# Splitting w_out by GpSimd ahead of time, through a spare tile and DRAM, in a fused attention and gated-MLP block

## The chip, the cores and the metric

The kernel runs on one core of a Trainium2 chip. The time is device microseconds (us) of one execution on that core; several executions were timed, and one further execution was taken by the hardware profiler. The engines are named as on the profile's page: PE (TensorE, matrix products), PEld (its weight loads), DVE (VectorE), ACT (ScalarE), POOL (GpSimd) and SP (SyncE, which here only issues transfers). A name with a q (SPq) is that engine's sequencer.

## What is computed

```python
x = A_x                                                # 1 x 2048 x 640, float32
h = x + _A_ref(_layernorm(x), A_wqkv, A_wo)            # 32 heads of 20, sliding window of 256
z = gelu(layernorm(h) @ w_in)                          # 2048 x 1728
z1, z2 = z[..., :864], layernorm(z[..., 864:])
g = w_sp @ z2 + b_sp[:, None]                          # w_sp: 2048 x 2048, over positions
h2 = h + (z1 * g) @ w_out                              # w_out: 864 x 640
```

Products want nearly full float32 accuracy. So the kernel writes an operand as a sum of two parts, a rounded "hi" (type fp32r) and the rest "lo" = raw - hi, and makes three products for one: hi x hi, hi x lo and lo x hi. To **split** a tile is to make these two parts.

## The kernel before

There are 16 row tiles of 128 positions. The attention half ends at about 550 us. Then come four stages, all written as a list of steps: `steps.append((products, what follows them))`, and `at(n, f)` hangs a piece of work f on step n.

- **z stage**, 64 steps (`z_pair`): z1 for all 16 tiles, from normalized rows that are read back from DRAM (`hn_d`). Rows of the last tiles (`hn(14)`, `hn(15)`) lie in `rows[2]` and `rows[3]`.
- **z2 stage, first five pairs**, 20 steps (`z2_pair(8..12)`): the second half of z (products `zb`), its layernorm, and `right_blocks`, which makes from it the seven pieces per block that a Strassen-like product with seven products instead of eight needs. Pieces are in tiles `ze` and `zl`. A part of these element-wise operations is given to GpSimd (`eng` = `nc.gpsimd`). The fifth pair is computed ahead and kept in DRAM (`z2_d`).
- **gate, opening half**, 56 steps (`first_gate`): the first 8 column tiles of w_sp times the pieces, products `g`, kept in DRAM as `g_d`. During it `staged_pieces` lets GpSimd alone make the seven pieces of the fifth pair through the spare tile `stage` [128, 2, 432]: load, copy (hi), subtract (lo), store to `zp_d`. SP loads them from there (lines 1019 and 1020).
- **z2, last three pairs**, 12 steps, **then the gate's second half**, 56 steps (`second_gate(0..7)`): products `g` again, added to `g_d`, times z1, turned (`turn_y`, products `yt_ps`), and projected with w_out (`final`, products `out_ps`).

The split w_out lies in `e1["wout"]`, in the memory that `win2` (the split w_in of the z2 stage) leaves at the last `zb` product. In the kernel before, `second_gate(0)` fills it: for each of the seven 128-row blocks, SP loads the raw block into `stage` (k < 4) or `rows[3]`, ACT copies it to the hi part (L136) and DVE subtracts (L137). Then `stage` and `rows[1]` serve as the two tiles of h that the result is added to (`load_h`, L1137).

The order within each engine in these stages is not written by hand. It is made when the program is built, by a scheduler that replays the steps on an estimated time line. So the same source lines can come in another order where the work around them changes. Every engine then takes its instructions strictly in that order, SP its transfers too.

Of the kernel before, what the change touches and what calls it, by code (L numbers as in the profile page):

```python
# [7 lines left out]
F32 = mybir.dt.float32  # L8
# [7 lines left out]
P = 128  # L16
S = 2048
D = 640
H = 32
DH = 20  # L20
NT = S // P
KD = D // P
FH = 864
KF = 7
HF = FH // 2
# [9 lines left out]
def block_kernel(ctx, tc, x, wqk, wv, wo, w_in, wsp, bsp, w_out, out):  # L35
    nc = tc.nc
# [4 lines left out]
    def pool(stack, name, **kw):  # L41
        return stack.enter_context(tc.tile_pool(name=name, bufs=1, reuse_waits="tile", **kw))

    const = pool(ctx, "const")
    dram = pool(ctx, "dram", space=DRAM)
# [12 lines left out]
    z2_d = dram.tile([2, P, FH], F32, name="z2_d")  # L58
    t_d = dram.tile([2, P, HF], F32, name="t_d")
    zp_d = dram.tile([7, P, 2, HF], F32, name="zp_d")  # L60

    ident = const.tile([P, P], F32, name="ident")
    nc.gpsimd.memset(ident, 1.0)
# [45 lines left out]
    def view(flat, lo, *shape):  # L109
        n = 1  # L110
        for d in shape:
            n *= d
        names = "abcd"[:len(shape)]
        return flat[:, lo:lo + n].rearrange(f"p ({' '.join(names)}) -> p {' '.join(names)}",
                                            **dict(zip(names, shape)))
# [15 lines left out]
    def m1(lo, *shape):  # L131
        return view(mem["m1"], lo, *shape)

    def split(hi, lo, raw, eng=None):

        nc.scalar.activation(hi, raw, AF.Copy)  # L136
        (eng or nc.vector).tensor_tensor(out=lo, in0=raw, in1=hi.bitcast(F32), op=OP.subtract)  # L137
# [91 lines left out]
    with ExitStack() as ab:  # L229
# [35 lines left out]
        minus = tmp2.tile([P, P], BF16, name="minus")  # L265
# [87 lines left out]
        def max_rows(g, b):  # L353


            n, cols, st = (40, 32)[b], m_cols.pop(b), slot_w[g % 3]
            m3 = tmp2.tile([P, 3, n], BF16, tag="m3", bufs=1, name=f"m3_{g}_{b}")
            mr = tmp2.tile([P, n], F32, tag="mr", bufs=1, name=f"mr{g}_{b}")
            nc.gpsimd.tensor_copy(out=m3[:, 0], in_=cols)
            nc.gpsimd.tensor_tensor(out=mr, in0=cols, in1=m3[:, 0], op=OP.subtract)  # L360
            nc.gpsimd.tensor_copy(out=m3[:, 1], in_=mr)
            nc.gpsimd.tensor_tensor(out=m3[:, 2], in0=mr, in1=m3[:, 1], op=OP.subtract)
            if b == 0:
                nc.gpsimd.tensor_copy(out=m_cols[1].rearrange("p (h r) -> p h r", h=4)[:, :, :2],
                                      in_=cols.rearrange("p (h r) -> p h r", h=4)[:, :, 8:])
            yield
            ps = s1_tile()[:3 * n, :P]
            nc.tensor.matmul(ps, m3.rearrange("p a c -> p (a c)"), minus, start=True, stop=True)
            mt = tmp2.tile([3 * n, P], BF16, tag="mt", bufs=1, name=f"mt{g}_{b}")
            nc.vector.tensor_copy(mt, ps)  # L370
            yield
            nc.sync.dma_start(st[b][0][120:123], mt.bitcast(F32))
            yield
# [86 lines left out]
        if True:  # L460
# [176 lines left out]
            for u in range(LEAD):  # L637
                for hh in range(4):
# [3 lines left out]
                    if (u, hh) in ((10, 0), (12, 2), (14, 0)):  # L642
                        rows = rows if u > 10 else max_rows(0, 0)
                        next(rows)
                    if (u, hh) == (NT, 0):
                        rows = max_rows(0, 1)
# [10 lines left out]
        for s in range(NU + 2):  # L657
# [7 lines left out]
            for hh in range(4):  # L665
# [4 lines left out]
                if hh == 0 and u1 <= NU and u1 % NT in (0, 10):  # L670
                    rows = max_rows((u1 - 1) // NT, 0 if u1 % NT else 1)
# [41 lines left out]
    def plus(out, a, b, op=OP.add, eng=None):  # L713
        (eng or nc.vector).tensor_tensor(out=out, in0=a, in1=b, op=op)  # L714

    def minus(out, a, b, eng=None):
        plus(out, a, b, OP.subtract, eng)
# [44 lines left out]
    def hn(i):  # L762
        if i % 4 < 2:
            return m1((4 + i % 2) * D, D)
        return rows[i % 4][:, :D] if i > 11 else view(fx, (i % 4 - 2 + i // 9 * 2) * D, D)

    def win_pieces(tiles):

# [39 lines left out]
    rows = [lp.tile([P, FH], F32, name=f"row{n}") for n in range(4)]  # L808
    stage = lp.tile([P, 2, HF], F32R, name="stage")
    tmp1 = lp.tile([P, 512], F32, name="tmp1")  # L810
    aw = lp.tile([P, 7168], F32R, name="aw")
    fx = lp.tile([P, 4096], F32, name="fx")
    win1 = win_pieces(zl)
    win2, zc, e1 = [], [], {}
# [31 lines left out]
    steps, later = [], {}  # L846

    def at(n, f):
        later.setdefault(n, []).append(f)
# [150 lines left out]
    def staged_pieces(n0, n1):  # L1000
        hi, raw = (stage.bitcast(F32)[:, k] for k in range(2))
        eng = nc.gpsimd
        b11, b12, b21, b22 = (z2_d[t, :, h * HF:(h + 1) * HF] for t in range(2) for h in range(2))

        def piece(m, src, less=None, keep=None):
            eng.dma_start(raw, src)
            if less is not None:
                eng.dma_start(hi, less)
                minus(raw, raw, hi, eng)
            if keep is not None:  # L1010
                eng.dma_start(keep, raw)
            eng.tensor_copy(out=stage[:, 0], in_=raw)
            minus(stage[:, 1], raw, hi, eng)
            eng.dma_start(zp_d[m], stage.bitcast(F32))

        for i, p in enumerate(((B11, b11), (T1, b12, b11, t_d[0]), (B21, b21), (T2, b22, t_d[0], t_d[1]), (B22, b22),
                               (T3, b22, b12), (T4, b21, t_d[1]))):
            at(n0 + 6 * i, lambda p=p: piece(*p))
        for i, m in enumerate((B11, T1, T2, B22, T3, B21, T4)):
            at(n1 + i + 1, lambda m=m: nc.sync.dma_start(zc[0][m].bitcast(F32), zp_d[m]))  # L1020

    e_start = []
    gbank = {}

# [108 lines left out]
    def tile_of(n):  # L1133
        return n // 2 + 8 * (n % 2)

    def load_h(n):
        nc.sync.dma_start(e1["h"][n % 2], h_d[tile_of(n)])  # L1137

    def final(n):
        ps = [bank("b", f"out_ps{n}_{j}") for j in range(2)]  # L1140
        project(ps, range(2), e1["y"])
        for j in range(2):
            final_half(ps, n, j, j == 1)
# [10 lines left out]
    def second_gate(p):  # L1154
        i, j = 2 * p, 2 * p + 1
        gi, gj = next(gate_rows), next(gate_rows)
        n0 = len(steps)
        if p == 0:
            at(n0, open_e1)
        g = {11: gi[:, :HF], 12: gi[:, HF:], 21: gj[:, :HF], 22: gj[:, HF:]}  # L1160

        def add(n):
            return lambda ps: plus(g[n], ps, g[n])

        def gated(n):
            t, c = (p + 8, j) if n > 20 else (p, i)
            z = e1["z1"][c % 2][:, HF * (n % 10 - 1):HF * (n % 10)]
            nc.vector.scalar_tensor_tensor(out=z, in0=g[n], scalar=bcol[:, t:t + 1], in1=z, op0=OP.add, op1=OP.mult)

        def load_z(n):  # L1170
            nc.sync.dma_start(e1["z1"][n % 2], z1_d[tile_of(n)])

        turns = (0, 1, 2, 3) if p > 1 else (0, 4, 4, 6)

        def extra(m):
            if p:
                for x, f in zip(turns, (lambda: turn_y(i - 2, e1["y"]), lambda: final(i - 2),
                                        lambda: turn_y(i - 1, e1["y"]), lambda: final(i - 1))):
                    if x == m:
                        f()  # L1180

        at(n0 - (0 if p else 1), lambda: nc.sync.dma_start(gi, g_d[p]))
        at(n0, lambda: nc.sync.dma_start(gj, g_d[p + 8]))
        at(n0 + (1 if p else 0), lambda: load_z(i))
        at(n0 + (turns[2] + 1 if p else 0), lambda: load_z(j))
        at(n0 + 4, lambda: gated(12))
        at(n0 + (6 if p == 1 else 5), lambda: gated(22))
        at(n0 + 6, lambda: gated(11))
        at(n0 + 7, lambda: gated(21))
        at(n0 + (9 if p == 0 else 6), lambda: load_h(i))  # L1190
        at(n0 + (11 if p == 0 else 7), lambda: load_h(j))
        gate_pair(p, 1, [add(11), add(22), add(12), add(12), add(22), add(11), add(21)], extra)
        if p == 0:
            def wout_raw(k):
                return e1["h"][0] if k < 4 else rows[3][:, :D]

            def load_wout(k):
                nc.sync.dma_start(wout_raw(k), w_out[k * P:(k + 1) * P, :])

            def put_wout(k):  # L1200
                split(e1["wout"][:, 0, k], e1["wout"][:, 1, k], wout_raw(k))

            for k in range(KF):
                t = n0 + (2 * k if k < 4 else 2 * k - 4)
                at(t, lambda k=k: load_wout(k))
                at(t + 2, lambda k=k: put_wout(k))

    for p in range(8):
        z_pair(p, 2 * p, 2 * p + 1, win1)
# [1 line left out]
        z2_pair(8 + p, p, p + 4, p)  # L1211
    z2_pair(12, 8, 12, 0, True)
    staged_pieces(len(steps) + 4, len(steps) + 49)
    for p in range(8):
        first_gate(p)
    for p in range(1, 4):
        z2_pair(12 + p, p + 8, p + 12, p)
    for p in range(8):
        second_gate(p)
# [56 lines left out]
    n = NT - 2  # L1276
# [34 lines left out]
```

## Time and profile before

| what | value |
|---|---|
| time, median of 3 runs | 1122.15 us (1116.82 to 1125.29) |
| profiled execution | 1121.05 us, its span 1119.3 us |
| PE busy | 1088.3 us, 97% of the span |
| DVE, ACT, POOL busy | 64%, 51%, 30% |
| granted TensorE clock | 0.998 of full |
| chain that ended last | PE 59%, DMA 5%, DVE 4%, ACT 2% |

Times in the views are us from the start of the span, durations in ns or us as marked. A view by stretches (windows) has one row for each stretch, with the busy time of each engine; the difference to the stretch's length is idle time. A timeline row has the start, the time from the first start to the last end, the engine, line, operation, tile written <- tiles read, and in brackets how long the engine had been idle and what ended that. The chain of waits is followed back from the last instruction.

### The profile page before, as it was taken

To read this page: it belongs to the slowest core of one execution; us is meant where nothing else is said; L and a number is where in the kernel's file an instruction comes from. 1 tells how busy PE (TensorE), PEld (TensorE's weight loads), DVE (VectorE), ACT (ScalarE), POOL (GpSimd) and SP (SyncE) were. 2 spreads that over 40 slices of the span, in tenths; PEclk is the share of its full clock that TensorE was granted. 3 is DMA by queue.
4 is the path that set the end of the run, shared out by engine and by line. 5 is a ranking of instruction groups with operands and counts; after the bars stand their busy time and mean duration, and the time that the engine had idled before them with its cause. 6 is when DMAs were issued, how large, how long until landed. Compare 5 with 4: busy or idle time off the path is not lost.

```text
span 1119.3 us, 27705 instructions
## 1 busy us (share of the span) xinstructions
PE 1088.3 (97%) x10667; PEld 976.1 (87%) x10667; DVE 715.4 (64%) x2038; ACT 573.9 (51%) x1222; POOL 336.4 (30%) x492
## 2 busy tenths in 40 slices
PE   8999999999999999989999999999999999999998
PEld 7998877668777887789989999999989899999998
DVE  6541113889999998676567478565538975566542
ACT  4334333259888999566766566433336521222210
POOL 3114444457666778401100155333101000000000
PEclk9999999999999999999999999999999999999999
DMA  7213665666666663588665421545571664444331
GB/s 259 74 33 102 171 218 165 204 208 196 194 198 192 209 194 119 170 277 288 226 200 177 151 76 38 182 153 197 177 248 38 202 182 140 124 135 148 99 95 59
DMA packets 86692, 182.44 MB, mean 163 GB/s; under 512 B 11552, under 2 KB 47904, under 8 KB 82640
## 3 DMA queue, kind: packets, MB, share of 16 engines
q1 hardware_dynamic: 82864, 169.46, 47.3%
q0 software_dynamic: 1392, 5.97, 1.6%
q10 hardware_dynamic: 2304, 5.24, 1.2%
q8 instruction: 84, 1.38, 0.5%
q14 instruction: 48, 0.39, 0.1%
HBM read 119.54 MB, written 62.29 MB: 162 GB/s over the span
## 4 chain that ended last, share of the span: by engine, by line
PE 59%; DMA 5%; DVE 4%; ACT 2%; issue 1%; SPq 1%; POOL 1%; DVEq 0%; ACTq 0%; POOLq 0%
PE g L1091 22%; PE out_ps L1130 8%; PE zb L953 7%; PE pv L432 5%; PE bank L338 4%; PE bank L404 4%; PE wo_ps L95 2%; PE zx L901 2%; PE zv L901 1%; PE zy L901 1%; PE yt_ps L1119 1%; DMA wraw<-w_in_in 1%; DMA fx<-w_in_in 1%; DVE zl L714 1%; DMA m<-r_d 1%
## 5 line engine op out<-in xcount | busy, mean ns | idle before, releaser
L407 ACT ACTIVATE pt<-bank 128x384 f32<-128x384 f32 (+2 forms) x512 | 200.2, 492 | 14.7 <-PE bank L404 10.9
L1091 PE MATMUL g<-zl,aw 128*128 128x432 f32 x768 | 172.4, 359 | 1.8 <-DVE zl L714 1.2
L720 ACT ACTIVATE aw<-fx 128x512 fp32r<-128x512 f32 (+2 forms) x160 | 93.0, 595 | 156.2 <-PE g L1091 98.7
L350 DVE CUSTOM_DVE_ANT_0 junk<-bank,strip 128x288 bf16<-128x288 f32 x392 | 157.7, 454 | 3.9 <-PE bank L338 2.4
L1091 PEld LDWEIGHTS g<-zl,aw 128*128 128x128 f32 x768 | 143.3, 188 | 9.1 <-DVE zl L714 1.8
L1091 PE MATMUL g<-ze,aw 128*128 128x432 f32 x576 | 133.8, 361 | 1.4 <-ACT aw L720 0.7
L432 PE MATMUL pv<-pt,v_sb 128*32 128x192 f32 (+3 forms) x1984 | 127.5, 321 | 3.0 <-DVE ot L448 1.3
L714 DVE TENSOR_TENSOR aw<-fx,aw 128x512 fp32r<-128x512 f32 (+2 forms) x152 | 98.7, 658 | 27.0 <-ACT aw L720 26.1
L1091 PEld LDWEIGHTS g<-ze,aw 128*128 128x128 f32 x576 | 107.2, 188 | 7.9 <-ACT aw L720 1.5
L404 PE MATMUL bank<-slot 123*32 123x288 bf16 (+5 forms) x1536 | 107.0, 280 | 2.8 <-ACT pt L407 1.3
L409 POOL TENSOR_SCALAR_AFFINE_SELECT pt<-pt 128x512 f32<-128x512 f32 x128 | 82.4, 644 | 49.6 <-ACT pt L407 48.5
L1130 PE MATMUL out_ps<-wout,y_sp 128*128 128x320 f32 (+1 forms) x630 | 95.9, 309 | 0.4 <-ACT y_sp L136 0.4
L953 PE MATMUL zb<-win,aw 128*128 128x432 f32 x480 | 95.4, 359 | 0.0
L1130 PEld LDWEIGHTS out_ps<-wout,y_sp 128*128 128x128 f32 (+1 forms) x630 | 94.0, 188 | 1.2 <-ACT y_sp L136 0.7
L953 PEld LDWEIGHTS zb<-win,aw 128*128 128x128 f32 x480 | 89.9, 188 | 4.9 <-DVE aw L714 0.4
L338 PE MATMUL bank<-slot 120*32 120x288 bf16 (+2 forms) x1264 | 87.7, 283 | 2.2 <-issue 1.2
L538 DVE TENSOR_TENSOR rest<-qk,sg 128x512 f32<-128x512 f32 x40 | 27.6, 691 | 86.5 <-ACT sg L536 86.5
L412 POOL TENSOR_SCALAR_AFFINE_SELECT pt<-pt 128x512 f32<-128x512 f32 x112 | 73.4, 655 | 0.0
L404 PEld LDWEIGHTS <-slot 123*32 123x32 bf16 x1536 | 53.6, 96 | 17.8 <-issue 6.9
L432 PEld LDWEIGHTS pv<-pt,v_sb 128*32 128x32 f32 x1984 | 60.2, 110 | 9.0 <-POOL pt L412 3.7
L541 POOL TENSOR_TENSOR sg<-rest,sg 128x512 bf16<-128x512 f32 x40 | 46.6, 1164 | 69.7 <-ACT sg L540 62.1
L714 DVE TENSOR_TENSOR row<-g,row 128x432 f32<-128x432 f32 x80 | 47.9, 602 | 27.9 <-PE g L1091 22.5
(210 smaller groups left out, 2158.3 us busy)
## 6 DMA issues: line engine op xcount, KB each, us to landing
fx<-wsp_in SPq DMA_DIRECT2D x32, 512.0 KB
slot<-qk_d SPq DMA_DIRECT2D x72, 200.0 KB
qk_d<-sg SPq DMA_DIRECT2D x32, 384.0 KB
slot<-qk_d SPq DMA_DIRECT2D x72, 160.0 KB
fx<-hn_d SPq DMA_DIRECT2D x32, 320.0 KB
o_d<-ot SPq DMA_DIRECT2D x64, 128.0 KB
z_d<-row SPq DMA_DIRECT2D x18, 432.0 KB
g_d<-row SPq DMA_DIRECT2D x16, 432.0 KB
```

What stands on the lines that cost most here:

```text
L338: nc.tensor.matmul(ps[32 * j:32 * j + 32, :n], part(st, half, 120, 0, hh, q0, 32), part(st, half, 120, 1, hh, lo + skip * j, n), start=Tru ...
L350: nc.vector.tensor_tensor_reduce(out=junk[:, :n], in0=ps[:, :n], in1=keep, scale=1.0, scalar=NEG, op0=OP.add, op1=OP.max, accum_out=m_cols ...
L404: nc.tensor.matmul(ps[32 * i:32 * i + 32, b:e], part(st, half, 123, 1, hh, k0, 32), part(st, half, 123, 0, hh, kb * P + b, e - b), start=T ...
L407: nc.scalar.activation(pt[:, hh, :n], ps[:, :n], AF.Exp, scale=SCALE)
L409: nc.gpsimd.affine_select(out=pt[:, :, :P], in_=pt[:, :, :P], pattern=[[0, 4], [1, P]], base=0, channel_multiplier=-1, compare_op=OP.is_ge ...
L412: nc.gpsimd.affine_select(out=pt[:, :, 256:], in_=pt[:, :, 256:], pattern=[[0, 4], [-1, P]], base=-1, channel_multiplier=1, compare_op=OP. ...
L432: nc.tensor.matmul(ps[32 * hh:32 * hh + 32, a - 512 * c:b - 512 * c], v_sb[:, kb, v0:v0 + 32], pt[:, hh, a - kb * P:b - kb * P], start=fir ...
L714: (eng or nc.vector).tensor_tensor(out=out, in0=a, in1=b, op=op)
L720: nc.scalar.activation(out, a, AF.Copy)
L953: nc.tensor.matmul(b[0][:, :HF], a[t][:, x, kk], win2[0][:, y, kk, h * HF:(h + 1) * HF], start=kk + x + y == 0, stop=kk == KD - 1 and x == 1)
L1091: nc.tensor.matmul(ps, w[m][x][:, k], zc[k][m][:, y], start=start and k + x + y == 0, stop=stop and k == 3 and x == 1, skip_group_check=True)
L1130: nc.tensor.matmul(ps[j][:, :HD], src[:w, a, k, :], e1["wout"][:w, b, k, j * HD:(j + 1) * HD], start=(k == 0 and a + b == 0), stop=(k == K ...
```

## The change

Four things are edited.

- A new function `staged_wout` makes both parts of 432 columns of w_out on GpSimd, through `stage`, in the manner of `staged_pieces`, and keeps them in a DRAM tensor `wout_d`. It is called for 11 chunks (ten of 432 columns, one of 160): seven at the z stage's steps 3, 11, ..., 51, four at the steps 130, 132, 134 and 136 (46 to 52 steps behind the 84 of the z and the first z2 stages, near the end of the gate's opening half), behind the seven staged pieces.
- `second_gate(0)` loads both parts of each block straight into `e1["wout"]`: seven transfers of 640 KB in place of seven of 320 KB, and no split.
- w_out is handed to the kernel as [128, 7 x 640], so that a chunk of columns is one run of memory in each partition.
- `hn(15)` lies in `stage` in place of `rows[3]`.

```diff
+    wout_d = dram.tile([P, 2, KF * D], F32, name="wout_d")
...
     def hn(i):
         if i % 4 < 2:
             return m1((4 + i % 2) * D, D)
-        return rows[i % 4][:, :D] if i > 11 else view(fx, (i % 4 - 2 + i // 9 * 2) * D, D)
+        if i == NT - 1:
+            return stage.bitcast(F32).rearrange("p a b -> p (a b)")[:, :D]
+        return rows[2][:, :D] if i == NT - 2 else view(fx, (i % 4 - 2 + i // 9 * 2) * D, D)
...
+    def staged_wout(c):
+        n = min(HF, KF * D - c)
+        hi, lo = (stage[:, k, :n] for k in range(2))
+        nc.gpsimd.dma_start(lo.bitcast(F32), w_out[:, c:c + n])
+        nc.gpsimd.tensor_copy(out=hi, in_=lo.bitcast(F32))
+        minus(lo, lo.bitcast(F32), hi.bitcast(F32), nc.gpsimd)
+        nc.gpsimd.dma_start(wout_d[:, :, c:c + n], stage.bitcast(F32)[:, :, :n])
...
         if p == 0:
-            def wout_raw(k):
-                return e1["h"][0] if k < 4 else rows[3][:, :D]
-
-            def load_wout(k):
-                nc.sync.dma_start(wout_raw(k), w_out[k * P:(k + 1) * P, :])
-
-            def put_wout(k):
-                split(e1["wout"][:, 0, k], e1["wout"][:, 1, k], wout_raw(k))
-
             for k in range(KF):
-                t = n0 + (2 * k if k < 4 else 2 * k - 4)
-                at(t, lambda k=k: load_wout(k))
-                at(t + 2, lambda k=k: put_wout(k))
+                at(n0 + 1 + 3 * k // 2, lambda k=k: nc.sync.dma_start(e1["wout"][:, :, k].bitcast(F32), wout_d[:, :, k * D:(k + 1) * D]))
...
+    for i, c in enumerate(range(0, KF * D, HF)):
+        at(3 + 8 * i if i < 7 else len(steps) + 32 + 2 * i, lambda c=c: staged_wout(c))
...
-    w_out = np.pad(np.asarray(B_w_out), ((0, KF * P - FH), (0, 0)))
+    w_out = np.pad(np.asarray(B_w_out), ((0, KF * P - FH), (0, 0))).reshape(KF, P, D).transpose(1, 0, 2)
+    w_out = w_out.reshape(P, KF * D)
```

The built programs show where this lands. The last number in a name is the tile's running number, which is one or more higher in the changed program, and line numbers grow by 1 to 11. First, DVE at the start of the gate's second half, where it makes the last pieces `zl` of the last z2 pair. Before:

```order
L714 TENSOR_TENSOR row2_9612<-row3_9613,row2_9612 128x432
L1168 SCALAR_TENSOR_TENSOR z1_0_13064<-row0_9610,bcol_81,z1_0_13064 128x432
L137 TENSOR_TENSOR wout_13062<-stage_9614,wout_13062 128x640
L714 TENSOR_TENSOR row3_9613<-row3_9613,row2_9612 128x432
L714 TENSOR_TENSOR zl11_9605<-row2_9612,zl11_9605 128x432
L714 TENSOR_TENSOR row1_9611<-g1_0_1_1_13097,row1_9611 128x432
L714 TENSOR_TENSOR aw_9616<-fx_9617,aw_9616 128x512
L714 TENSOR_TENSOR zl15_9609<-row3_9613,zl15_9609 128x432
```

The same place in the changed program:

```order
L715 TENSOR_TENSOR row2_9613<-row3_9614,row2_9613 128x432
L1179 SCALAR_TENSOR_TENSOR z1_0_13109<-row0_9611,bcol_82,z1_0_13109 128x432
L715 TENSOR_TENSOR row3_9614<-row3_9614,row2_9613 128x432
L715 TENSOR_TENSOR row1_9612<-g1_0_1_1_13142,row1_9612 128x432
L715 TENSOR_TENSOR aw_9617<-fx_9618,aw_9617 128x512
L715 TENSOR_TENSOR zl11_9606<-row2_9613,zl11_9606 128x432
L715 TENSOR_TENSOR aw_9617<-tmp1_9616,aw_9617 128x512
L715 TENSOR_TENSOR zl15_9610<-row3_9614,zl15_9610 128x432
```

The subtraction of w_out is gone, and the add to `row1` and the first `aw` part, which stood behind the piece `zl11`, now stand ahead of it. PE, which consumes the pieces, moved as well. Before:

```order
L1091 MATMUL g1_0_1_1_13097<-zl10_9604,aw_9616 128x432 x2
L1119 MATMUL yt_ps0_0_13228<-ident_76,z1_0_13064 128x128 x3
L1091 MATMUL g1_0_0_0_13072<-zl11_9605,aw_9616 128x432 x3
L1091 MATMUL g1_0_1_1_13097<-ze3_10529,aw_9616 128x432 x3
L1091 MATMUL g1_0_1_1_13097<-ze10_10536,aw_9616 128x432 x3
L1091 MATMUL g1_0_1_1_13097<-zl5_9599,aw_9616 128x432 x3
L1091 MATMUL g1_0_1_1_13097<-zl12_9606,aw_9616 128x432 x3
L1091 MATMUL g1_1_1_1_13253<-ze1_10527,aw_9616 128x432 x2
```

And now:

```order
L1102 MATMUL g1_0_1_1_13142<-zl10_9605,aw_9617 128x432 x2
L1130 MATMUL yt_ps0_0_13264<-ident_77,z1_0_13109 128x128 x3
L1102 MATMUL g1_0_0_0_13116<-zl11_9606,aw_9617 128x432
L1102 MATMUL g1_1_1_1_13285<-ze1_10528,aw_9617 128x432 x2
L1102 MATMUL g1_0_1_1_13142<-ze3_10530,aw_9617 128x432 x3
L1102 MATMUL g1_0_1_1_13142<-ze10_10537,aw_9617 128x432 x3
L1102 MATMUL g1_0_1_1_13142<-zl5_9600,aw_9617 128x432 x3
L1102 MATMUL g1_0_1_1_13142<-zl12_9607,aw_9617 128x432 x3
L1102 MATMUL g1_0_0_0_13116<-zl11_9606,aw_9617 128x432 x2
L1102 MATMUL g1_1_1_1_13285<-ze1_10528,aw_9617 128x432
```

The lo part of `zl11` is read by the second of the rows that name `zl11`: before, all three products with it came in one block; now one product comes first, then fourteen others, then the two that remain. Last, SP from the loads of g and z1 on. Before:

```order
L1182 DMA row0_9610<-g_d_71 128x864
L1171 DMA z1_0_13064<-z1_d_69 128x864
L1171 DMA z1_1_13065<-z1_d_69 128x864
L1183 DMA row1_9611<-g_d_71 128x864
L1041 DMA fx_9617<-wsp_in 128x1024 x2
L1198 DMA stage_9614<-w_out_in 128x640 x2
L1182 DMA row2_9612<-g_d_71 128x864
L1198 DMA row3_9613<-w_out_in 128x640
L1198 DMA stage_9614<-w_out_in 128x640
L1198 DMA row3_9613<-w_out_in 128x640
L1183 DMA row0_9610<-g_d_71 128x864
```

Now:

```order
L1193 DMA row0_9611<-g_d_71 128x864
L1182 DMA z1_0_13109<-z1_d_69 128x864
L1182 DMA z1_1_13110<-z1_d_69 128x864
L1194 DMA row1_9612<-g_d_71 128x864
L1206 DMA wout_13107<-wout_d_76 128x2x640 x2
L1052 DMA fx_9618<-wsp_in 128x1024 x2
L1206 DMA wout_13107<-wout_d_76 128x2x640 x5
L1193 DMA row2_9613<-g_d_71 128x864
L1193 DMA row3_9614<-g_d_71 128x864
L1194 DMA row0_9611<-g_d_71 128x864
```

Two of the seven loads of `wout` stand ahead of the w_sp tiles of `second_gate(2)` (`wsp_in x2`), five behind them and ahead of the g rows of `second_gate(1)` (`row2`). The load of h into `stage` also moved: it was between the raw loads, and now stands some 20 transfers earlier, among the loads of the staged pieces (`ze6`, then `stage<-h_d`, then `ze3`).

## The prediction

> **What bounds the kernel now.** First the page's engine shares (PE busy for 97% of the span), then the view by stretches over the stages that the edit touches:
>
> ```profile
> core 0: us, PE busy (x) PEld busy (x) DVE busy (x) ACT busy (x) POOL busy (x), PEclk, DMA share, GB/s
> 583.00:641.00 58.00, 57.68 (x295) 55.22 (x295) 35.18 (x74) 35.31 (x66) 1.60 (x1) 1.00 0.52 169
> 698.00:770.00 72.00, 72.00 (x368) 68.82 (x367) 44.46 (x74) 30.13 (x54) 22.34 (x30) 1.00 0.49 167
> 770.00:832.00 62.00, 60.91 (x309) 57.32 (x308) 31.33 (x49) 21.79 (x39) 9.11 (x10) 1.00 0.63 205
> 868.00:890.00 22.00, 19.84 (x98) 17.32 (x97) 19.59 (x39) 13.31 (x22) 1.10 (x2) 1.00 0.61 209
> 890.00:910.00 20.00, 20.00 (x116) 19.34 (x115) 16.84 (x30) 6.50 (x12) 0.00 (x0) 1.00 0.61 185
> ```
>
> The first row is the z stage, the next two the gate's opening half, the last two the start of its second half, where the split of w_out stands. PE is full nearly everywhere. From 868 to 890 it idles for 22.00 - 19.84 = 2.16 us, while DVE is busy for 19.59 of the 22 us. The waits of PE from 867 to 912 and the chain of waits (start, us, what) say why:
>
> ```profile
> PE g L1091 <- DVE zl L714: 1.2, 2, 1.0
> PE g L1091 <- ACT zl L720: 0.6, 1, 0.6
> PE g L1091 <- ACT aw L720: 0.3, 1, 0.3
> ...
> 870.11 0.74 DVE wout L137
> 870.85 0.12 DVE mvz L977
> 870.97 0.09 DVE mvz L983
> ...
> 871.14 1.00 ACT row L985
> ...
> 881.49 0.59 DVE row L714
> ...
> 882.09 0.53 DVE zl L714
> ...
> 882.66 14.35 PE g L1091 x71
> ```
>
> PE waits 1.2 + 0.6 + 0.3 = 2.1 us here for pieces (`zl`) and w_sp parts, and the chain runs through DVE, with one subtraction of w_out on it. From 882.66 on PE is the chain itself. So this place can give **at most 2.2 us**, 0.2% of the time, whatever is taken off DVE and ACT. A change of over 1% (11 us, about what a measurement of this kernel can tell from no change) can only be a loss.
>
> **What the change removes.** Seven splits: seven ACT copies and seven DVE subtractions. From the view of the tile `wout` (min/median/max ns), and DVE's timeline:
>
> ```profile
> L137 DVE TENSOR_TENSOR wout<-stage,wout x4: 810/815/819, 870.0 to 892.0; 128x640 fp32r<-128x640 f32 x4
> 880.76 0.81 DVE L137 TENSOR_TENSOR wout<-stage,wout 128x640 fp32r<-128x640 f32 x1
> 881.49 0.59 DVE L714 TENSOR_TENSOR row<-row,row 128x432 f32<-128x432 f32 x1
> 882.66 0.66 PE L1091 MATMUL g<-zl,aw 128*128 128x432 f32 x2 [1.02 <-DVE zl L714]
> ```
>
> Back to back one subtraction holds DVE for 881.49 - 880.76 = 0.73 us, seven for 5.1 us. Only two stand ahead of PE's last stall: the one at 870.11, which holds up the layernorm factors (L977, L983) that ACT's normalization at 871.14 waits for, and the one at 880.76, which holds up the last pieces. Behind them PE has no stall, so the other five are worth nothing by themselves, nor are ACT's copies, since ACT has idle time here (13.31 of 22 us busy). Removed from the path: 0.74 + 0.73 = **1.5 us**.
>
> Two moves bear on the second of these. `zl11` now stands behind an add (0.52 us back to back) and an `aw` part (0.60), so it is ready at 882.6 - 1.47 + 1.12 = 882.25, not 881.1. But PE now has 14 other products between the first product with `zl11` and those that need its lo part, 14 x 0.196 = 2.7 us (72 us for 368 products), which covers it. What is late next is the hi part of a w_sp tile, which PE takes right behind the first product with `zl11`; ACT can make it only once PE has let go of its buffer, and I leave 0.1 to 0.6 us of stall there. So I keep 1.5 us, with bounds 0 and 2.2.
>
> **What it adds on the DMA queue.** Seven loads of 655 KB in place of seven of 328 KB, so 2.3 MB more, and their places change. The transfer rate where the queue is full:
>
> ```profile
> 868.00:877.00 9.00, 7.86 (x38) 6.52 (x37) 6.58 (x17) 6.45 (x11) 1.10 (x2) 1.00 0.94 342
> 886.62 0.59 DVE L714 TENSOR_TENSOR row<-g,row 128x432 f32<-128x432 f32 x1
> ```
>
> At 342 GB/s the four loads of g and z1 (1.77 MB), two of `wout` (1.31) and two of w_sp for `second_gate(2)` (1.05) take 12.1 us from 868.2 on, to 880.3. The first DVE operation on that w_sp is the sum into `tmp`, by the order some 11 us behind the start of the last pieces, at about 883 to 884: in time by 3 us. The other five `wout` (3.28 MB) end at 889.9, the g row of `second_gate(1)` at 891.2. Its add ran at 886.62 in the kernel before; in the new order it stands behind 32 DVE operations from 873.0 on, 17.9 us at their back-to-back times, so DVE reaches it at about 890.9. A wait of 0.3 us, up to 2 if the rate is lower; behind it DVE queues the parts of y and of w_sp for PE, but DVE is spared five more subtractions of w_out between 885 and 901, 3.6 us. Cost 0, bounds 0 and +2. If that cover is gone, PE waits for y.
>
> **What it adds on GpSimd.** 11 chunks of load, copy, subtract, store: the form of a staged piece with one input, which the timeline shows twice here:
>
> ```profile
> 710.48 0.76 POOL L1006 DMA_DIRECT2D stage<-z_d  x1 [4.76 <-DMA z_d<-row]
> 713.53 1.04 POOL L1012 CAST stage<-stage 128x432 fp32r<-128x432 f32 x1 [2.28 <-DMA stage<-z_d]
> 714.66 1.12 POOL L714 TENSOR_TENSOR stage<-stage 128x432 fp32r<-128x432 f32 x1
> 716.09 0.56 POOL L1014 DMA_DIRECT2D zp_d<-stage  x1 [0.31 <-POOL stage L714]
> 719.12 0.55 POOL L1006 DMA_DIRECT2D stage<-z_d  x1 [2.47 <-DMA zp_d<-stage]
> ...
> 734.47 0.55 POOL L1006 DMA_DIRECT2D stage<-z_d  x1 [2.44 <-DMA zp_d<-stage]
> ...
> 746.33 0.55 POOL L1006 DMA_DIRECT2D stage<-z_d  x1 [5.59 <-DMA zp_d<-stage]
> ```
>
> From load to next load 719.12 - 710.48 = 8.6 us, or 11.9 where the store is slow; from load to the subtraction's end 5.3. GpSimd doesn't follow PE's steps, it runs its list as fast as its waits allow. Behind the chunks stand z2's `aw` parts, so GpSimd must be through in time:
>
> ```profile
> 559.84 0.27 PE L841 MATMUL ht_b<-ident,row 128*128 128x128 f32 x1
> 630.57 1.60 POOL L714 TENSOR_TENSOR aw<-fx,aw 128x640 fp32r<-128x640 f32 x1 [74.99 <-ACT aw L720]
> 635.58 1.34 PE L953 MATMUL zb<-win,aw 128*128 128x432 f32 x6
> 639.12 1.14 PE L953 MATMUL zb<-win,aw 128*128 128x432 f32 x5
> ...
> 792.14 0.33 SPq L1198 DMA_DIRECT2D stage<-w_out_in  x1
> 825.60 2.03 SPq L1020 DMA_DIRECT2D ze<-zp_d  x2
> 831.98 35.88 PE L953 MATMUL zb<-win,aw 128*128 128x432 f32 x180
> 833.01 1.56 POOL L714 TENSOR_TENSOR aw<-fx,aw 128x640 fp32r<-128x640 f32 x1 [43.22 <-DMA g_d<-row]
> ```
>
> Seven chunks in the z stage: `stage` is free of `hn(15)` at about 560.3, when PE has turned it. The seventh subtraction ends at 560.3 + 6 x 8.6 + 5.3 = 617, or 637 at 11.9 per chunk. GpSimd sat idle from 555 to 630.57 before. PE needs the `aw` part for the pair's second tile behind 30 `zb` products, 11 of which are done at 640.1; with 19 more from 641.3 that is 645.0. So there are 6 us to spare in the worse case.
>
> Four chunks behind the staged pieces: `stage` came free at 792.14 (SP's raw load waited for just that). Three chunks and a short one of about 7 us to the landing of its store end at 825 to 835. Two queues wait behind them. GpSimd's `aw` part (833.01) is needed behind 30 products from 831.98, at 837.9. And SP now has the load of h into `stage` right behind the `ze` load of 825.60: it waits for the last store, 0 to 9 us, and holds the transfers behind it, the next normalized rows (`fx<-hn_d`) among them. Those serve PE from 60 products behind 831.98 on, 843.7. So both are in time, and I cost them at nothing, with +2 as the upper bound.
>
> DVE's cover: a tensor operation of GpSimd can hold up one on DVE. In the z2 stage one 128x432 subtraction took 1.87 us, not 0.6, beside such an operation:
>
> ```profile
> 850.78 1.82 POOL L714 TENSOR_TENSOR aw<-fx,aw 128x640 fp32r<-128x640 f32 x1 [3.17 <-ACT aw L720]
> 851.19 1.87 DVE L714 TENSOR_TENSOR ze<-row,ze 128x432 fp32r<-128x432 f32 x1
> ```
>
> [...] What counts is whether PE feels it: the z stage would get 14 such operations at up to 1.3 us, 18 us at most on 35.18 of 58 us of DVE time, so 53 of 58. The stretch 698 to 770 has the same pieces (22.34 us of GpSimd) beside a DVE as busy (44.46 of 72), and PE is at 72.00 of 72.00. I take 0.3 us, bounds 0 and +3.
>
> **The sum.** -1.5 + 0.3 = -1.2 us on the profiled execution's 1121.05 us (span 1119.3 and 1.75 around it): 1119.9. That execution lay 1.1 us below the median of the runs shown, 1122.15, so for a median I say **1120.9 us**.
>
> **The rivals.**
> - *The wait moves to the DMA queue.* The five `wout` loads hold up the g rows and DVE takes back what it gained: no change, 1122 to 1123. For it: the margin worked out above is about 0. Against: DVE is spared 5.1 us in all by 901.
> - *GpSimd is late* (the slower side). The place is z2's first `aw` part, the price one PE stall. It decides where a chunk takes over (645.0 - 560.3 - 5.3 - 0.6 - 1.6) / 6 = 12.9 us. At 14 PE loses 6.8 us at 645 and about 2 at 838: 1120.9 + 8.9 = 1130. For it: the longest store wait was 5.59 us, and the queue is as full in the z stage (share 0.52). Against: no one-input piece took over 11.9.
> [...]
> - *The change gives all it can:* PE's 2.16 us go whole, 1120.0. This is inside the forecast's own range.
> - *It does not do what it says:* the scheduler's other moves (the z stage's products come in another order) eat the gain: 1122 to 1125.
>
> **How the numbers follow.** Chances: forecast with its bounds (1119.9 to 1122) 0.55, DMA queue 0.15, GpSimd late 0.10, lock 0.08, other moves 0.12. The three runs before spread over 8.5 us, so a median moves by some us by itself. The forecast's side reaches down to 1119.9 - 4.4 = 1115.5, half of that spread, the upper ends of lock and moves with the same noise to 1128; the late GpSimd at 1130 is left out. Faster by over 1% 0.01 (PE has no 11 us to give), slower by over 1% 0.05 (half of the late GpSimd), the rest the same.
>
> **What would show it.** Right: no `wout` subtraction on DVE; PE's idle time from 868 to 890 falls from 2.16 to about 0.7; PE still full in the z stage, with GpSimd busy for some 10 to 16 us more there; `stage` through by 835. Wrong: a PE wait on a GpSimd `aw` part near 645 or 838, an SP transfer waiting past 835, or a DVE wait on `row<-g_d` near 890 followed by one of PE on y.

## The result, and the profile after

| kernel | median | executions | ratio to before |
|---|---|---|---|
| before | 1119.62 us (1114.68 to 1125.29) | 20 | |
| after | 1126.51 us (1121.96 to 1131.23) | 20 | 1.0056, interval 1.0041 to 1.007 |

The change makes the kernel slower, by about 0.6% or 6.9 us, where the prediction had it 1.2 us faster. The interval is clear of 1, so these runs tell apart much less than the 1% that the prediction took for the limit. The profiled execution of the changed kernel took 1131.23 us, 10.2 us more than the one of before (1121.05 us), so the traces differ by more than the medians do.

The view by stretches of the changed kernel:

```profile
core 0: us, PE busy (x) PEld busy (x) DVE busy (x) ACT busy (x) POOL busy (x), PEclk, DMA share, GB/s
583.00:641.00 58.00, 58.00 (x298) 55.58 (x297) 37.00 (x72) 33.95 (x65) 16.73 (x21) 1.00 0.71 234
...
770.00:832.00 62.00, 58.28 (x293) 54.37 (x292) 33.22 (x47) 20.07 (x37) 18.78 (x24) 1.00 0.65 208
832.00:868.00 36.00, 35.30 (x179) 32.96 (x178) 16.97 (x33) 14.00 (x24) 9.74 (x10) 1.00 0.43 144
868.00:890.00 22.00, 15.76 (x69) 13.47 (x68) 18.97 (x44) 14.57 (x25) 1.65 (x3) 0.92 0.50 181
```

The place that was to gain has lost: from 868 to 890 PE idles for 6.24 us, where it idled for 2.16. The stretch ahead, 832 to 868, shows how it began: DVE is busy for 16.97 us. In the kernel before it was 25.74:

```profile
832.00:868.00 36.00, 36.00 (x183) 33.95 (x182) 25.74 (x54) 21.07 (x37) 7.42 (x7) 1.00 0.25 86
```

So 21 DVE operations are missing there (33 against 54). Part of that is only a later start: PE's `zb` products of the last z2 pairs begin at 836.18 in this profile and began at 831.98 in the one of before, 4.2 us earlier. Counted from that start, DVE does 41 operations in 36 us (busy for 19.29 us from 836.20 to 872.20), so 13 are missing, while PE does its products without a break. They come later, and PE then waits for them. PE's waits of the changed kernel from 830 to 912:

```profile
PE g L1102 <- ACT zl L721: 5.3, 2, 5.0
PE g L1102 <- ACT row L960: 1.1, 1, 1.1
PE g L1102 <- DVE row L715: 0.7, 1, 0.7
```

These are 7.1 us against 2.1 before. The last of them, at 833.72, stands ahead of the `zb` products, and the kernel before has the same wait at 829.52, just outside this window. So the fair comparison is 6.4 us against 2.1, or 4.3 us more. The chain of waits tells why DVE is late. It is followed back here from PE's products right behind the 5.0 us wait, which ends at 883.75; short pieces between these, of 0.33 us at most, are left out:

```profile
836.33 1.12 POOL stage L715
837.75 2.43 DMA wout_d<-stage
840.24 0.32 SPq L1148
840.65 0.40 SPq L1023
...
842.11 0.93 SPq L965
843.45 5.86 DMA fx<-hn_d
849.41 0.75 ACT aw L721
850.22 1.58 POOL aw L715
851.80 0.52 POOL mvz L982
...
882.13 1.11 ACT row L988
883.24 0.46 ACT zl L721
883.72 0.62 DVE zl L715
884.39 6.97 PE g L1102 x26
```

The last chunk of w_out is stored at 837.75, the store lands at 840.2, and only then SP goes on: it issues the load of h into `stage` (L1148), which waited for the store, and 1.9 us later the normalized rows (`fx<-hn_d`). SP's timeline in the changed kernel, and its wait from 800 to 915:

```profile
829.81 0.41 SPq L1023 DMA_DIRECT2D ze<-zp_d  x1
840.24 0.32 SPq L1148 DMA_DIRECT2D stage<-h_d  x1
...
842.11 1.71 SPq L965 DMA_DIRECT2D fx<-hn_d  x2
```

```profile
SPq L1148 <- DMA wout_d<-stage: 9.9, 2, 7.3
```

In the kernel before, the same two rows were issued 10.6 us earlier, or 6.4 us earlier when both are counted from the start of PE's `zb` products:

```profile
831.50 1.71 SPq L962 DMA_DIRECT2D fx<-hn_d  x2
```

ACT takes the rows first, at 849.41, and its next operation follows at 850.05. Its timeline in the changed kernel, and DVE's:

```profile
849.41 0.74 ACT L721 ACTIVATE aw<-fx 128x640 fp32r<-128x640 f32 x1 [8.87 <-DMA fx<-hn_d]
850.05 0.94 ACT L960 ACTIVATE row<-zb 128x432 f32<-128x432 f32 x2
```

```profile
850.60 0.61 DVE L978 BATCH_NORM_STATS2 stz<-row 128x6 f32<-128x432 f32 x1 [9.42 <-ACT row L960]
```

ACT stands idle for 8.87 us at the copy of a row that PE does not need yet. Behind that copy in ACT's order stand the copies of finished products (`row<-zb`), and DVE waits 9.42 us for those: DVE's next work is the statistics of the pair in hand. GpSimd is held by the same copy: its `aw` part needs it, and behind that part stands its step of the layernorm (`mvz`, L982), which in the chain comes last of the two, by 0.2 us. In the kernel before, the copy that stands behind that of the row ran at 838.81, 11.2 us earlier (7.0 us from the start of `zb`):

```profile
838.17 0.74 ACT L720 ACTIVATE aw<-fx 128x640 fp32r<-128x640 f32 x1 [1.82 <-PE zb L953]
838.81 0.51 ACT L957 ACTIVATE row<-zb 128x432 f32<-128x432 f32 x1
```

### The profile page after: what moved, and what is told of

Read it like the earlier page. It is cut to its first block, busy times and chain, and to the rows that moved or that the text cites. A ratio compares the mean times of both kernels' runs of the same rounds, so it can differ in the third digit from the quotient of the medians.

```text
span 1129.5 us, 27735 instructions
## 1 busy us (share of the span) xinstructions
PE 1092.0 (97%) x10667; PEld 977.3 (87%) x10667; DVE 718.6 (64%) x2031; ACT 567.6 (50%) x1215; POOL 371.2 (33%) x536
## 4 chain that ended last, share of the span: by engine, by line
PE 59%; DMA 16%; DVE 7%; POOL 6%; issue 5%; ACT 3%; SPq 2%; POOLq 0%; DVEq 0%; ACTq 0%
PE g L1102 11%; PE out_ps L1141 8%; PE pv L433 6%; PE bank L339 5%; PE bank L405 5%; DMA zp_d<-stage 2%; PE wo_ps L96 2%; PE qk L523 2%; PE qk L525 2%; PE qk L524 2%; DMA stage<-z_d 2%; DMA qk_d<-sg 2%; PE zx L904 2%; POOL stage L715 2%; DMA wout_d<-stage 2%
## 5 line engine op out<-in xcount | busy, mean ns | idle before, releaser
L721 ACT ACTIVATE aw<-fx 128x512 fp32r<-128x512 f32 (+3 forms) x160 | 92.7, 595 | 187.6 <-PE g L1102 114.1
L1102 PEld LDWEIGHTS g<-zl,aw 128*128 128x128 f32 x768 | 144.4, 189 | 12.8 <-ACT zl L721 5.9
L715 DVE TENSOR_TENSOR aw<-fx,aw 128x512 fp32r<-128x512 f32 (+3 forms) x152 | 102.3, 685 | 27.6 <-ACT aw L721 27.2
L405 PE MATMUL bank<-slot 123*32 123x288 bf16 (+6 forms) x1536 | 106.0, 282 | 2.3 <-ACT pt L408 1.7
```

Source lines behind the costliest of these rows:

```text
L405: nc.tensor.matmul(ps[32 * i:32 * i + 32, b:e], part(st, half, 123, 1, hh, k0, 32), part(st, half, 123, 0, hh, kb * P + b, e - b), start=T ...
L721: nc.scalar.activation(out, a, AF.Copy)
L1102: nc.tensor.matmul(ps, w[m][x][:, k], zc[k][m][:, y], start=start and k + x + y == 0, stop=stop and k == 3 and x == 1, skip_group_check=True)
```

## The experiments

Theory **A**: SP's load of h into `stage` waits for the last staged store, and what stands behind it on SP comes too late for ACT and DVE. Its rivals: **B**, the chunks themselves cost (transfers, GpSimd, its lock on DVE: in the kernel before, a DVE subtraction beside an operation of GpSimd took 1.87 us and not 0.6); **C**, other transfers do, the load of h at its new place or the doubled loads of `wout`. Each expectation spells its theories out. Ratios are to the kernel before, run beside them.

**The load of h moved back (h_later).** An ACT operation of one column writes `stage` in `second_gate(0)`, so that the scheduler puts SP's load of h behind the loads of `wout`. Nothing else moves: in the two traces every other transfer of SP and every other instruction of GpSimd, DVE and ACT stands in the same order.

```diff
         if p == 0:
+            at(n0 + 5, lambda: nc.scalar.activation(stage.bitcast(F32)[:, 0, :1], e1["z1"][0][:, HF:HF + 1], AF.Copy))
             for k in range(KF):
```

> The changed kernel with one edit: a copy of one column from z1 into stage (ACT, one element per partition) at the gate's second half, so that the load of h into stage cannot be placed among the ze loads; in SP's order only that load moves, behind the w_out loads. All staging stays. Theory A (SP's load of h waited for the last store of the staged chunks, 830 to 840 us, and held the fx<-hn_d loads behind it, which ACT waited 8.9 us for): SP issues the last fx<-hn_d at about 833 to 836 instead of 842 to 844, ACT's wait for them falls below 2 us, PE's wait on the zl pieces falls from 5.0 to about 1 us, and the ratio to before falls from 1.0056 to about 1.000 to 1.002. Rival B (the transfers and GpSimd operations of the four late chunks slow the neighbouring transfers and operations): ratio stays at 1.004 to 1.006. Rival C (the doubled w_out loads hold up the g rows and w_sp tiles behind 868 us): ratio stays at 1.004 to 1.006, with DVE waiting for row<-g_d near 890.

Measured: 1118.54 us, ratio 0.9996 (0.9974 to 1.0018). PE has its time back, with the same chunks and the same loads of `wout`:

```profile
832.00:868.00 36.00, 36.00 (x184) 34.27 (x183) 26.48 (x57) 21.33 (x37) 6.57 (x8) 1.00 0.25 83
868.00:890.00 22.00, 21.29 (x106) 18.81 (x105) 18.71 (x37) 10.27 (x19) 0.55 (x1) 1.00 1.00 380
```

PE is at 21.29 of 22 us while the transfers run at 380 GB/s, so neither the doubled loads nor the chunks cost what was lost there. The late chunks may not be quite free: at its first `zb` product PE waits 1.0 us for an `aw` part whose rows landed late (1.1 us in h_later_again), and no kernel without late chunks has this wait. No run separates its cause. One doubt stayed: in this profile the chunks also ended earlier, with the last store at 829.02 and not 837.75.

**A 32 KB load in its place (tiny_wait).** It is h_later with one transfer more, which nothing uses, on the spot in SP's order where the changed kernel has the load of h. Every other instruction keeps its place.

```diff
+    at(len(steps) + 52, lambda: nc.sync.dma_start(stage.bitcast(F32)[:, 0, :64], h_d[0][:, :64]))
     for p in range(8):
         first_gate(p)
```

> This is h_later (the changed kernel with the load of h moved behind the loads of wout in SP's order) with one transfer more: a load of 64 columns (32 KB), never used, into stage, standing in SP's order exactly where the changed kernel has the load of h. Every other instruction of every engine keeps its place. If SP's wait for the last staged store is the cause (A), nearly the whole loss comes back for 32 KB: the small load waits until the last wout_d store has landed (831 to 840 us), fx<-hn_d stands behind it, PE is down to 16 to 19 of 22 us from 868 to 890, and the ratio to before is 1.002 to 1.007. If the loss came from the bytes moved or from the late chunks' traffic (B), or from the load of h colliding with other loads there (C), it stays as h_later, 0.998 to 1.001.

Measured: 1129.31 us, ratio 1.0081 (1.0052 to 1.011). The whole loss is back for 32 KB, somewhat more than the expected upper end of 1.007, by the middle value. Four views of tiny_wait follow: SP's wait, SP's timeline, ACT's timeline, and the stretch from 868 on:

```profile
SPq L1217 <- DMA wout_d<-stage: 10.0, 2, 7.9
```

```profile
837.77 0.32 SPq L1217 DMA_DIRECT2D stage<-h_d  x1
...
839.63 1.70 SPq L965 DMA_DIRECT2D fx<-hn_d  x2
```

```profile
847.09 0.74 ACT L721 ACTIVATE aw<-fx 128x640 fp32r<-128x640 f32 x1 [9.03 <-DMA fx<-hn_d]
```

```profile
868.00:890.00 22.00, 15.75 (x63) 13.32 (x62) 18.08 (x39) 13.18 (x24) 1.65 (x3) 0.84 0.61 222
```

Here the load of h itself goes at 900. What costs is the wait in SP's queue, and not the bytes behind it.

**The two kernels once more, beside it (after_again, h_later_again).**

> The changed kernel itself, beside the others on the same chip, for a second profile: its first one was its longest execution. Both theories: ratio 1.004 to 1.007. A: whenever the last wout_d store lands after about 831 us, the load of h and fx<-hn_d go that late, and the time lost by PE from 868 to 890 grows with that lateness; in an execution shorter than the first the store lands earlier and the loss there is smaller.

> h_later once more, as the twin of tiny_wait on the same chip. A and B both: 0.998 to 1.001, PE at 21 of 22 us from 868 to 890. Its last store landed at about 831 in its first profile, near where the held loads would have gone anyway; if it lands later here with no loss, the wait alone is what costs, and if a loss appears with the store late and nothing held, A falls.

Measured: after_again 1130.24 us, ratio 1.0103 (1.0075 to 1.013); h_later_again 1120.04 us, ratio 1.0015 (0.9999 to 1.003). The interval of after_again lies above that of the first result (1.0041 to 1.007), so the size of the loss differs between the two sets of runs; why is not known. On the same chip tiny_wait lies 9.3 us above its twin h_later_again. In h_later_again the last store was issued at 830.04, and SP issued its rows at 831.42, as the kernel before did; so no profile shows the store as late as 837 with nothing held. Counted from the start of `zb` (831.21), though, that store landed 3.2 us later (830.04 and 4.4 to landing), and the one of tiny_wait 4.0 us later (835.27 and 2.4, with `zb` at 833.71). So a store that is nearly as late, with nothing held behind it, costs nothing of this size. How fast the loss grows with the lateness is not shown either: both held profiles lie close together (PE busy for 15.76 and 15.69 of 22 us).

**Less staging (h_later_7, no_staging).** Both keep the changed loads of `wout` and replace chunks by copies of raw w_out from DRAM to DRAM on GpSimd's queue; the split of these columns is left out. h_later_7 replaces the last four chunks (and has h_later's line), no_staging all eleven.

```diff
+    def copied_wout(c):
+        for k in range(2):
+            nc.gpsimd.dma_start(wout_d[:, k, c:], w_out[:, c:])
...
-        at(3 + 8 * i if i < 7 else len(steps) + 32 + 2 * i, lambda c=c: staged_wout(c))
+    at(72, lambda: copied_wout(0))
```

> As h_later, but the four late chunks are not staged: their columns of wout_d get the raw w_out in both parts by two transfers from DRAM to DRAM during the z2 stage, so the lo part of those columns is left out of the computation. The seven chunks of the z stage and the second half's loads stay. Theory A: within 2 us of h_later (ratio to before 0.998 to 1.001). Rival B: clearly below h_later, by 4 to 6 us. Rival C: as h_later, 1.004 to 1.006.

> The changed kernel without any staged chunk: both parts of wout_d get the raw w_out by two transfers from DRAM to DRAM during the z2 stage, so the split itself is left out of the computation, and the second half loads wout_d as in the changed kernel. stage is free from about 792 us on, so the load of h in its early place waits for nothing. Theory A with the prediction's first term: the split's removal alone gives 1.5 us, ratio to before about 0.9985. Rival C (the doubled loads take it back or more): 1.000 to 1.005. If GpSimd's chunks in the z stage cost PE something, this is faster than h_later_7 by that.

Measured: 1123.47 us, ratio 1.0037 (1.0016 to 1.0057), and 1131.46 us, ratio 1.0098 (1.0067 to 1.0129). Both were badly made. The copies depend on nothing, so the scheduler put them at the very start, among the loads that the attention half begins with. GpSimd's timeline and the first stretch of no_staging, and that stretch of before:

```profile
2.83 1.28 POOL L1035 DMA_DIRECT2D wout_d<-w_out_in  x2
```

```profile
0.00:100.00 100.00, 84.25 (x544) 78.58 (x544) 46.96 (x121) 31.84 (x74) 19.50 (x35) 0.91 0.46 148
```

```profile
0.00:100.00 100.00, 97.01 (x624) 90.19 (x625) 48.06 (x123) 38.58 (x87) 25.55 (x38) 1.00 0.36 113
```

PE loses 12.8 us there in no_staging and 2.3 in h_later_7 (94.70 busy), none of it where the change is. At 868 to 890 no_staging has PE at 21.28 of 22 us, which fits A, but the whole times of these two say nothing on the question.

**Seven chunks alone (z_chunks_alone).** The kernel before with seven chunks from w_out to `wout_d` at the z stage's steps, which nothing reads. With `stage` free from the start, the scheduler let them run early, the last two at the start of the z stage: they ran from 473.54 (first load) to 571.07 (last store).

```diff
+    for i in range(7):
+        at(3 + 8 * i, lambda i=i: staged_wout(i, stage))
```

> The kernel before, plus seven staged chunks on GpSimd through stage at the z stage's steps 3 to 51, whose results are read by nobody; the split in the second half stays as before. Theory A: the z stage has room for them, ratio 0.999 to 1.001, PE full from 583 to 641. Rival of the lock or the queue in the z stage: 1.002 to 1.005, with PE waits on DVE, ACT or GpSimd between 560 and 650.

Measured: 1117.66 us, ratio 0.9976 (0.9957 to 0.9996). Early chunks cost nothing. Five of the seven were stored before the z stage, which begins at 550.96 here, so on chunks inside it this run says little; the changed kernel's own profile does, below.

**All chunks early (early_all), and its twin (chunks_unread).** early_all is the changed kernel with `hn(15)` back in `rows[3]` and all eleven chunks at steps 0, 4, ..., 40, so that none is late. chunks_unread is the kernel before with the same eleven chunks, unread, and w_out still split by ACT and DVE.

```diff
-        at(3 + 8 * i if i < 7 else len(steps) + 32 + 2 * i, lambda c=c: staged_wout(c))
+        at(4 * i, lambda c=c: staged_wout(c))
```

> The changed kernel with hn(15) back in its row tile and all 11 chunks called from the first step of the z stage on, every fourth step, so that stage is free of them long before the staged pieces, and the load of h behind the staged pieces waits for nothing late. w_out is split and read as in the changed kernel. A: SP issues fx<-hn_d near 830, PE is at 21 or more of 22 us from 868 to 890, and the term of -1.5 us for the two subtractions stands alone: ratio 0.996 to 1.000, about 0.9987. B (the chunks cost by themselves, by GpSimd, by the DMA queue or by doubled loads of wout): 1.002 to 1.006 wherever the chunks stand. A further risk under both: chunks that run past 630 us hold up z2's first aw part on GpSimd, then PE waits there and the ratio rises by 0.001 for each us.

> The changed kernel with all chunks early, once more beside its twin without the change. If the two subtractions taken off DVE's path are worth their 1.5 us, it is 0.0013 below chunks_unread (1 to 2 us), and PE is at 21 or more of 22 us from 868 to 890, against 19.8 to 20.0 in the twin. If the early chunks themselves make a kernel faster (they change the order of other work too), both are alike, near 0.9976.

> The kernel before with the same 11 chunks called at the same early steps, from w_out to wout_d, which nothing reads: the raw loads, copies and subtractions of w_out in the second half stay. If the early chunks are free and the removal is what gains: ratio 0.999 to 1.001, PE at 19.8 to 20.0 of 22 us from 868 to 890. If the chunks' own effect on the order is what made z_chunks_alone and early_all 0.9976: 0.997 to 0.998 here too.

Measured: early_all 1116.56 us, ratio 0.9976 (0.9958 to 0.9995), and again 1118.21 us, ratio 0.9991 (0.9976 to 1.0006); chunks_unread 1118.98 us, ratio 0.9986 (0.9968 to 1.0004). With the late chunks gone the changed kernel lies 13.7 us, or 1.2%, below after_again, which ran beside the first early_all. Against the kernel before, it gains nothing that the times can tell: the twin, which has the chunks without the change, is as fast. What the change saves is seen in PE's waits. From 830 to 912, first chunks_unread, then the second early_all:

```profile
PE g L1100 <- DVE zl L715: 1.2, 2, 1.0
PE g L1100 <- ACT zl L721: 0.5, 1, 0.5
PE g L1100 <- ACT aw L721: 0.3, 1, 0.3
```

```profile
PE g L1100 <- ACT zl L721: 0.5, 1, 0.5
PE g L1100 <- ACT aw L721: 0.3, 1, 0.3
PE g L1100 <- DVE zl L715: 0.2, 1, 0.2
```

1.0 us of wait on DVE's `zl` goes with the subtractions, and nothing else. The expectation of PE at 19.8 to 20.0 of 22 us from 868 to 890 for chunks_unread did not come out (20.98, against 20.97 in early_all_again): its `zb` products begin at 823.97, 8 us ahead of those of the kernel before, and half of its idle time falls ahead of 868 (PE busy for 34.98 of 36 us from 832 on).

**All profiles from one point on.** What stands ahead of the last `zb` products differs by up to 16.6 us between profiles (they begin at 823.97 in chunks_unread, at 840.59 in no_staging), and by 4.2 us between the two of early_all. From their start to the end of the span the profiles fall into three groups:

| group | kernels | us from the start of `zb` to the end |
|---|---|---|
| w_out split in the second half | before, z_chunks_alone, chunks_unread | 287.3, 287.2, 287.2 |
| no split there, SP not held | h_later twice, early_all twice, h_later_7, no_staging | 285.8, 286.3, 286.1, 286.1, 286.2, 285.9 |
| no split there, SP held | after, after_again, tiny_wait | 293.3, 294.7, 294.7 |

So what the change removes is worth 0.9 to 1.5 us, and SP's wait costs 7.0 to 8.9. The middle group holds kernels with late chunks, with early ones and with none, so behind this point the chunks make no difference, and all six have the doubled loads.

## Why the prediction was wrong

- **The step that failed** is the last of "What it adds on GpSimd": "it waits for the last store, 0 to 9 us, and holds the transfers behind it ... So both are in time, and I cost them at nothing, with +2 as the upper bound". The wait and what it holds were named. What was wrong is whom the held rows were late for. They were measured against PE's need, and PE never waited for them, as its row shows:

```profile
836.18 35.87 PE L956 MATMUL zb<-win,aw 128*128 128x432 f32 x180
```

  (That need was even put too early. Three of the six tiles are loaded ahead of the held rows, so PE needs those 90 products behind its start and not 60: at 849.6, where the prediction has 843.7.) But ACT's copy of these rows stands ahead of the copies that DVE's statistics wait for, and GpSimd's part of them ahead of its step of the layernorm. From there a chain of statistics, normalization and pieces leads to the products from 875 on, where PE had waits already. A delay of 6.4 us, counted from PE's start, came out as 4.3 us more of waiting (6.4 against 2.1) and a slower clock behind it (granted 0.92 from 868 to 890, 1.00 before).
- **The end of the chunks** was a second wrong size. They were to be through "at 825 to 835" and ended at 840.2, because they began 4 us later (796.19, not 792.14) and took up to 15.3 us from load to load (805.66 to 820.96), where I had 8.6 to 11.9 from a stretch in which the loads and stores of GpSimd's queue landed in 2.9 and 2.7 us, in the middle. Beside the loads for the z2 stage they took:

```profile
wout_d<-stage POOLq DMA_DIRECT2D x3, 432.0 KB, 6.1
stage<-w_out_in POOLq DMA_DIRECT2D x3, 216.0 KB, 3.9
```

- **What the sum did not hold at all** is a drop of the granted clock after the wait (0.50 from 884 to 886), some 2 us (below). Of the 10.2 us between the two traces, 6.0 lie behind the start of `zb` (293.3 against 287.3): 4.3 us of waits and 2.1 of clock, by these views, make 6.4. The other 4.2 lie ahead of it, 3.3 of them as idle time of PE from 770 to 868 (3.72 + 0.70 against 1.09 + 0). Their cause is open. The largest of these waits, 1.58 us at 822.49 for an add of DVE, stands ahead of SP's wait, so that wait can't be its cause; after_again and tiny_wait have it at the same product (1.61 and 1.30 us), the two profiles of h_later do not. Two profiles of early_all, one and the same program without late chunks, have 2.80 and 1.09 us of idle time from 770 to 832, so a part of it comes and goes by itself.
- **The removal** was right in place and a little large: -1.5 us by the sum; in the runs -1.0 us of wait on `zl`, and -0.9 to -1.5 us from the start of `zb` to the end. PE's idle time from 868 to 890, said to fall from 2.16 to about 0.7, was 0.71 and 1.19 in the two profiles of h_later and 0.76 and 1.03 in those of early_all.
- **The z stage** was right: PE is at 58.00 of 58 us with GpSimd at 16.73, the seven chunks end at 632.9, and z2's first `aw` part on GpSimd follows at 633.84. That was closer than the prediction had it: from load to load three of the six took 12.3 to 13.6 us, where 11.9 was the longest row, and only the mean of 11.2 kept them below its limit of 12.9. The lock cost PE nothing there: with the chunks DVE was busy for 37.00, 39.05 and 35.88 of the 58 us (after, after_again, tiny_wait; 35.18 before), and PE for 58.00 each time. So no run shows the sum's +0.3 for it, which was the author's estimate, nor what its chance of 0.08 stood for. The rival of the scheduler's other moves falls as well: h_later has all of them and is no slower than the kernel before (ratio 0.9996).
- **The DMA queue** as a rival falls: with the queue at a share of 1.00 from 868 to 890, h_later loses nothing behind it (PE 20.00 of 20 us from 890 to 910).
- **"GpSimd is late"** named the right neighbourhood on the slower side and the wrong path: GpSimd's own `aw` part was to decide at 645 or 838, but SP's queue did, and PE never waited for a part of GpSimd's there. "An SP transfer waiting past 835" was named as a sign of being wrong, and it is the one that came.

## What to carry to other kernels

When a transfer takes over a buffer that another engine frees late, look at what stands behind it in the issuing engine's order, and then at what stands behind *those* on the engines that receive them, and not only at when the last consumer needs the data. Here the delay went on to work that never touches the late rows: ACT waited 8.87 us for them, and DVE 9.42 us for the copies behind them in ACT's order. Such a wait is cheap to find: put a small transfer with the same wait in the same place, or move the one that waits, and compare.

## What the runs showed of the hardware

Behind PE's wait of 5.04 us its granted clock was 0.50 (884 to 886). PE's timeline in the changed kernel around the wait, and the granted clock in the stretch from 884 to 888:

```profile
877.37 1.33 PE L1102 MATMUL g<-zl,aw 128*128 128x432 f32 x6
883.75 2.09 PE L1102 MATMUL g<-zl,aw 128*128 128x432 f32 x4 [5.04 <-ACT zl L721]
885.84 1.09 PE L1102 MATMUL g<-ze,aw 128*128 128x432 f32 x2
886.73 1.08 PE L1102 MATMUL g<-zl,aw 128*128 128x432 f32 x3
887.65 1.35 PE L1102 MATMUL g<-ze,aw 128*128 128x432 f32 x6
```

```profile
884.00:888.00 4.00, 3.87 (x11) 2.87 (x11) 4.00 (x9) 2.04 (x5) 0.00 (x0) 0.57 1.02 388
```

The nine products from 883.75 to 887.65 take 3.90 us, 0.43 each; at the 0.196 us of the prediction they would take 1.8. So the wait costs up to 2.1 us more than it lasts. In the finer view the clock is at 0.50 from 884 to 886 and at 1.00 from 888 on. after_again and tiny_wait have the same wait of 5.0 us and a granted clock of 0.84 from 868 to 890; there the products stay slow for 6.1 and 7.0 us. The kernel before, whose waits there are of 1.0 us at most, has 1.00, and so has the changed kernel from 770 to 832 with its wait of 1.58 us.

The load of the last late chunk (80 KB) on GpSimd's queue took longer where SP's queue was at work beside it, 6.2 us against 2.6. First the changed kernel, where SP was held, then h_later, where it was not (us from issue to landing last):

```profile
stage<-w_out_in POOLq DMA_DIRECT2D x1, 80.0 KB, 2.6
```

```profile
stage<-w_out_in POOLq DMA_DIRECT2D x1, 80.0 KB, 6.2
```

The other profiles agree: 2.8 and 3.2 us in after_again and tiny_wait, with SP held, and 5.8 in h_later_again. Size decided less here: the three loads of 216 KB of the same h_later profile took 2.8 us in the middle.
